# Decode attention beside a small dense block: a nested TensorE loop that works the V cache batch by batch

## The chip, the cores and the metric

One Trainium2 chip, one core. The metric is the device time of one execution in microseconds (us). It has a part outside the profiled span of the core (here 1.7 to 3 us).

## The reference, cut to what matters

Two batches, one query position, 32 heads, 4096 cached keys and values of 128 elements, all bf16. Attention (A) is mixed with a two-layer ReLU block (B) by a sigmoid gate.

```python
q = (x @ wq)                                            # 2 x 32 heads x 128
scores = jnp.einsum("bhqd,bhkd->bhqk", q, k_cache) * (128 ** -0.5)
p = softmax(scores)                                     # over 4096 keys
o = jnp.einsum("bhqk,bhkd->bhqd", p, v_cache)
a = o @ wo                                              # ... heads joined before
b = relu(x @ w1) @ w2
return g * a + (1 - g) * b                              # g = sigmoid(sum(x * gate_w))
```

K and V are 64 MiB each. They are read once, so the work is a stream of memory: 64 loads of 2 MB (two heads of one batch each), 32 of K and then 32 of V.

## The kernel before

A small recording layer keeps a list of instructions for each engine, works out the semaphore waits and emits them; TensorE's repeated parts stand in a loop of 8 turns of 4 loads. One queue (sync engine) issues all big loads into four slots of 2 MB, so that a load waits until TensorE is done with the load four places earlier:

```python
    def kv_in(n):                                       # load n: K for n < 32, then V
        c = A_k_cache if n < 32 else A_v_cache
        hp, b = divmod(n % 32, 2)                       # the two batches alternate
        return c[b, 2 * hp:2 * hp + 2].rearrange("h (p r) d -> (h p) r d", p=64)
    ...
    for n in range(64):
        waits = []
        if n >= NSLOT:                                  # NSLOT = 4
            prev = n - NSLOT
            waits.append(f"T_{prev}_7" if prev < 32 else f"pv_{prev - 32}")
        load(f"ld_kv_{n}", kv_sb[:, n % NSLOT, :, :], kv_in(n), waits=waits, sem=f"slot{n % NSLOT}")
```

In the K part TensorE transposes each load (64 transposes, evacuated by VectorE and ScalarE) and multiplies by q; the scores of both batches stay in PSUM. Then comes the turn from K to V: for each batch the row maximum, the exponential, 16 transposes of the probabilities back into PSUM; then the sums of both batches; and only then the pV loop. Each pV is 64 matmuls with a load of V as the stationary side and a column pair of probabilities (`pst`) as the moving side; VectorE stages `pst` (`stage_p`) and scales each result (`o_norm`).

```python
    for g in range(2):                                  # both batches before the first pV
        row_max(g)
        exps(g)
        ptrans(g)
    denom_l(0)
    stage_p(0)
    denom_l(1)
    for i in (2, 1, 3):
        stage_p(i)
    denom()                                             # sums and reciprocals of both batches
    P.begin_loop(NIT)
    for p in range(PER):
        PV(p)
    P.end_loop()
    for i in range(32):
        o_norm(i)
        if i + PER < 32:
            stage_p(i + PER)
    ...
    def stage_p(i):
        hp, g = divmod(i, 2)
        ...
        for hh in range(2):
            P.add("dve", lambda e, hh=hh: e.tensor_copy(out=pst[64 * hh:64 * hh + 64, p, :, hh], in_=src[:, :, 2 * hp + hh]),
                  waits=[f"pt_{g}", "c_ps"] + ([f"pv_{i - PER}"] if i >= PER else []),
                  signal=f"pst_{i}" if hh else None, sem=f"ps{p}")

    def o_norm(i):
        hp, g = divmod(i, 2)
        P.add("dve", lambda e: e.tensor_tensor(out=oT[:, g, 2 * hp:2 * hp + 2], in0=o_col(i % PER), in1=rg[:, g, 2 * hp:2 * hp + 2], op=ALU.mult),
              waits=[f"pv_{i}", f"rg_{g}"], signal=f"oT_{i}", sem=f"on{i % PER}")
```

(The sum, the gate and the output projection, whose weights are the last 4 MB to be loaded, are cut here.)

## Time and profile before

| | before |
|---|---|
| time at the prediction (3 runs) | 352.36 us median (351.13, 352.36, 573.64; the last is no fast run) |
| span of the profiled run | 349.2 us |
| bytes read | 145.4 MB |
| DMA rate in the K part, in the V part | 428, 429 GB/s |
| TensorE busy in the K part, in the V part | 99.7%, 39% |

The lines of the page of the kernel before that show this, in 40 equal slices of the span; the digits are the DMA engines' mean busy share in tenths, the numbers what they moved:

```profile
DMA  8999999999999999999999999999999999999994
GB/s 338 405 415 428 430 424 422 434 428 424 425 435 426 423 430 434 428 424 434 430 424 423 381 422 439 426 422 430 434 428 421 432 430 428 424 435 428 424 420 167
```

DMA is full from end to end. In slice 23 (192 to 201 us) the rate dips to 381 GB/s. The same place in stretches of 1 us, then the turn from K to V as a whole and the V part (columns: busy us with instruction counts of TensorE's matmuls, its weight loads, VectorE, ScalarE and GpSimd, then granted TensorE clock, DMA share, GB/s):

```profile
194.00:195.00 1.00, 1.00 (x44) 1.00 (x42) 0.33 (x2) 0.00 (x0) 0.00 (x0) 0.50 0.99 410
195.00:196.00 1.00, 1.00 (x43) 1.00 (x41) 0.53 (x3) 0.00 (x0) 0.00 (x0) 0.50 0.60 229
196.00:197.00 1.00, 0.63 (x24) 0.54 (x21) 0.00 (x0) 0.00 (x0) 0.00 (x0) 0.50 1.04 295
197.00:198.00 1.00, 0.98 (x35) 0.98 (x36) 0.53 (x3) 0.00 (x0) 0.00 (x0) 0.50 0.78 279
198.00:199.00 1.00, 1.00 (x44) 1.00 (x42) 0.00 (x0) 0.00 (x0) 0.00 (x0) 0.50 1.15 492
180.00:210.00 30.00, 18.64 (x465) 16.74 (x462) 13.28 (x52) 5.82 (x8) 0.00 (x0) 0.64 0.99 412
204.00:318.00 114.00, 43.91 (x1522) 42.52 (x1523) 12.54 (x72) 0.00 (x0) 0.00 (x0) 0.50 1.01 429
```

Three stretches from 195 to 198 us are at about two thirds of the rate; 412 against 428 GB/s over 30 us is 30 * (1 - 412/428) = 1.1 us. The cause is in the timeline of the kernel before (start, duration, engine, line, operation; the bracket is idle time and what ended it):

```profile
182.49 1.29 DVE L353 COPY kt_sb<-PS 128x1024 bf16<-128x1024 bf16 x2 [0.20 <-PE PS L326]
...
186.42 1.23 DVE L373 TENSOR_REDUCE m<-PS 128x1 f32<-128x1024 f32 x1
186.42 1.11 ACT L386 ACTIVATE E<-PS,negM 128x1024 bf16<-128x1024 f32 x1 [2.03 <-DVE negM L381]
...
187.68 1.18 PE L392 MATMUL PS<-ident,E 128*64 128x128 bf16 x16 [3.24 <-ACT E L386]
...
189.15 1.11 ACT L386 ACTIVATE E<-PS,negM 128x1024 bf16<-128x1024 f32 x1 [1.52 <-DVE negM L381]
...
190.41 1.91 PE L392 MATMUL PS<-ident,E 128*64 128x128 bf16 x16 [1.55 <-ACT E L386]
...
192.25 1.06 PE L402 MATMUL PS<-lm,ones 128*128 128x32 f32 x4
...
193.13 3.50 PE L433 MATMUL PS<-pst,kv_sb 128*128 128x2 bf16 x125
...
195.04 0.16 DVE L423 TENSOR_TENSOR oT<-PS,rg 128x2 bf16<-128x2 f32 x1 [0.70 <-PE PS L433]
```

The last K transposes are evacuated by 183.8 us. Batch 0's exponential runs at 186.4, its transposes at 187.7; then TensorE waits for batch 1's exponential (189.15), transposes it (190.4) and makes the sums (192.25). pV 0 is over at about 195.0, where VectorE scales it (the line at 195.04), and only then is the fifth V load issued. Each V load after that waits on TensorE for nothing: TensorE waits about 3 us for each load (lines of the timeline in the middle of V):

```profile
262.74 1.87 PE L433 MATMUL PS<-pst,kv_sb 128*128 128x2 bf16 x64 [2.96 <-DMA kv_sb<-in_A_v_cache_dram]
267.72 1.85 PE L433 MATMUL PS<-pst,kv_sb 128*128 128x2 bf16 x64 [3.11 <-DMA kv_sb<-in_A_v_cache_dram]
272.62 1.85 PE L433 MATMUL PS<-pst,kv_sb 128*128 128x2 bf16 x64 [3.05 <-DMA kv_sb<-in_A_v_cache_dram]
277.52 0.64 PE L433 MATMUL PS<-pst,kv_sb 128*128 128x2 bf16 x19 [3.05 <-DMA kv_sb<-in_A_v_cache_dram]
```

Three lines of the page's list of DMA queues, on which no reading rested at first and everything rests later:

```profile
q1 hardware_dynamic: 10488, 145.43, 98.4%
q8 instruction: 7, 0.11, 0.1%
q14 instruction: 5, 0.04, 0.0%
```

### The profile page before, as it was taken

The numbers are of one execution on the slowest core, as the hardware profiler recorded it, in microseconds if no ns is written. First come the engines' busy times: TensorE is split into PE (matmuls) and PEld (weight loads), VectorE is DVE, ScalarE is ACT, GpSimd is POOL, SyncE is SP. The second block draws the span as 40 slices with busy tenths as digits, with TensorE's granted clock in tenths as the row PEclk, the third lists the DMA queues.
The fourth block names the chain that finished last, engine by engine and source line by source line (L and its number), as shares of the span: only waits on it lengthen the run. The fifth ranks groups of instructions, "written<-read, shape, count | busy, mean of one in ns | idle before, by whom it ended". The sixth has DMA issues, their size and how long they took to land.

```text
span 349.2 us, 10866 instructions
## 1 busy us (share of the span) xinstructions
PE 236.4 (68%) x5019; PEld 202.6 (58%) x5019; DVE 132.0 (38%) x293; ACT 99.5 (28%) x105; POOL 12.0 (3%) x52
## 2 busy tenths in 40 slices
PE   2549999999999999999994933443244433443244
PEld 0549888787888788787883823443234423443233
DVE  1004766676766676666767311110111011110010
ACT  1004656565665566555763000000000000000000
POOL 5000000000000000000000000000000000000000
PEclk9999999999999999999997555555555555555555
DMA  8999999999999999999999999999999999999994
GB/s 338 405 415 428 430 424 422 434 428 424 425 435 426 423 430 434 428 424 434 430 424 423 381 422 439 426 422 430 434 428 421 432 430 428 424 435 428 424 420 167
DMA packets 10514, 145.59 MB, mean 417 GB/s; under 512 B 1187, under 2 KB 1286, under 8 KB 1670
## 3 DMA queue, kind: packets, MB, share of 16 engines
q1 hardware_dynamic: 10488, 145.43, 98.4%
q8 instruction: 7, 0.11, 0.1%
q14 instruction: 5, 0.04, 0.0%
q10 hardware_dynamic: 14, 0.00, 0.0%
HBM read 145.43 MB, written 0.00 MB: 416 GB/s over the span
## 4 chain that ended last, share of the span: by engine, by line
PE 51%; DMA 43%; DVE 2%; issue 2%; SPq 1%; ACT 0%; DVEq 0%
PE PS L326 35%; DMA kv_sb<-in_A_v_cache_dram 29%; PE PS L337 10%; DMA wo_sb<-in_A_wo_dram 7%; DMA kv_sb<-in_A_k_cache_dram 7%; PE PS L433 5%; SPq L236 1%; DVE m L373 1%; PE PS L392 1%; DVE kt_sb L353 0%; ACT E L386 0%; DVE mq L376 0%; DVE negM L381 0%; PE PS L402 0%; PE PS L484 0%
## 5 line engine op out<-in xcount | busy, mean ns | idle before, releaser
L326 PEld LDWEIGHTS PS<-ident,kv_sb 128*128 128x128 bf16 x2048 | 117.3, 99 | 18.7 <-issue 14.4
L326 PE MATMUL PS<-ident,kv_sb 128*128 128x128 bf16 x2048 | 124.2, 222 | 3.7 <-DMA kv_sb<-in_A_k_cache_dram 3.4
L353 DVE COPY kt_sb<-PS 128x1024 bf16<-128x1024 bf16 x160 | 105.4, 688 | 55.6 <-PE PS L326 55.6
L433 PE MATMUL PS<-pst,kv_sb 128*128 128x2 bf16 x2048 | 59.2, 165 | 85.8 <-DMA kv_sb<-in_A_v_cache_dram 82.4
L350 ACT ACTIVATE kt_sb<-PS 128x1024 bf16<-128x1024 bf16 x96 | 94.1, 1022 | 69.2 <-PE PS L326 69.2
L433 PEld LDWEIGHTS PS<-pst,kv_sb 128*128 128x128 bf16 x2048 | 57.4, 104 | 87.7 <-issue 69.0
L423 DVE TENSOR_TENSOR oT<-PS,rg 128x2 bf16<-128x2 f32 x32 | 5.1, 159 | 128.0 <-PE PS L433 128.0
L337 PE MATMUL PS<-kt_sb,qst 128*32 128x512 bf16 x512 | 38.2, 382 | 0.0
L337 PEld LDWEIGHTS PS<-kt_sb,qst 128*32 128x32 bf16 x512 | 13.3, 95 | 12.5 <-DVE kt_sb L353 3.6
L417 DVE COPY pst<-PS 64x64 bf16<-64x64 bf16 x64 | 14.3, 224 | 2.1 <-PE PS L392 1.4
L357 POOL COPY qst<-qmask 128x64 bf16<-128x64 bf16 x32 | 7.4, 237 | 151.7 <-PE PS L337 140.6
L484 PE MATMUL PS<-wo_sb,os_sb 128*2 128x128 bf16 x128 | 4.3, 305 | 3.2 <-DMA wo_sb<-in_A_wo_dram 3.2
L302 PE MATMUL PS<-xT_sb,wq_sb 128*128 128x2 bf16 x128 | 3.6, 165 | 4.2 <-DMA wq_sb<-in_A_wq_dram 4.2
L392 PE MATMUL PS<-ident,E 128*64 128x128 bf16 x32 | 3.1, 272 | 4.8 <-ACT E L386 4.8
L302 PEld LDWEIGHTS PS<-xT_sb,wq_sb 128*128 128x128 bf16 x128 | 3.5, 104 | 4.2 <-DMA wq_sb<-in_A_wq_dram 4.2
L392 PEld LDWEIGHTS PS<-ident,E 128*64 128x64 bf16 x32 | 2.6, 142 | 5.5 <-ACT E L386 5.5
L484 PEld LDWEIGHTS PS<-wo_sb,os_sb 128*2 128x2 bf16 x128 | 2.9, 112 | 4.4 <-DMA wo_sb<-in_A_wo_dram 2.2
L286 PE MATMUL PS<-ident,gw_sb 1*128 1x1 bf16 x4 | 0.3, 172 | 4.4 <-DMA gw_sb<-in_gate_w_dram 4.4
L386 ACT ACTIVATE E<-PS,negM 128x1024 bf16<-128x1024 f32 x2 | 2.2, 1113 | 3.6 <-DVE negM L381 3.6
L307 DVE TENSOR_SCALAR qmask<-PS 128x32 bf16<-128x32 f32 x2 | 0.5, 323 | 7.4 <-PE PS L302 7.4
L448 ACT ACTIVATE hr_sb<-PS 128x20 f32<-128x20 f32 x1 | 0.2, 187 | 10.2 <-PE PS L442 10.2
L516 DVE TENSOR_TENSOR out_sb<-PS,f_sb 98x128 bf16<-98x128 f32 x1 | 0.3, 291 | 7.2 <-PE PS L484 7.2
(51 smaller groups left out, 31.5 us busy)
## 6 DMA issues: line engine op xcount, KB each, us to landing
kv_sb<-in_A_k_cache_dram SPq DMA_DIRECT2D x32, 2048.0 KB, 14.5
kv_sb<-in_A_v_cache_dram SPq DMA_DIRECT2D x32, 2048.0 KB, 17.6
wq_sb<-in_A_wq_dram SPq DMA_DIRECT2D x1, 4096.0 KB, 12.4
wo_sb<-in_A_wo_dram SPq DMA_DIRECT2D x1, 2048.0 KB, 22.1
w_sb<-in_B_w_dram SPq DMA_DIRECT2D x1, 1376.0 KB, 15.3
w_sb<-in_B_w_dram SPq DMA_DIRECT2D x1, 1280.0 KB, 18.9
wo_sb<-in_A_wo_dram SPq DMA_DIRECT2D x1, 1024.0 KB, 24.1
wo_sb<-in_A_wo_dram SPq DMA_DIRECT2D x1, 512.0 KB, 24.9
```

Source lines behind the costliest of these rows:

```text
L236: P.add(eng, lambda e: e.dma_start(dst, src), waits=waits, signal=name, sem=sem or name, inc=16)
L302: P.add("pe", lambda e, h=h, t=t: e.matmul(bank(7, 2 * h, 2), lhsT=wq_sb[:, t, h * 128:(h + 1) * 128], rhs=xT_sb[:, t, :], start=(t == 0), ...
L326: P.add("pe", lambda e, iv, q=q, rr=rr, r=r: e.transpose(bank16(4 + q % 4, rr * 128, 128), kv_sb[:, p, r, :], ident16[:, :]), waits=waits ...
L337: P.add("pe", lambda e, iv, c=c, hh=hh: e.matmul(S_chunk(p % 2, c), lhsT=qst[:, p, hh, :], rhs=kt_sb[:, p % NKT, 8 * c:8 * c + 8, 64 * hh: ...
L350: P.add("act", lambda e, dst=dst, src=src: e.activation(out=dst, in_=src, func=ACT.Copy), waits=w, signal=f"ev_{i}_{q}", sem=f"ev{p}{q}")
L353: P.add("dve", lambda e, dst=dst, src=src: e.tensor_copy(out=dst, in_=src), waits=w, signal=f"ev_{i}_{q}", sem=f"ev{p}{q}")
L357: P.add("pool", lambda e: e.tensor_copy(out=qst[:, p, :, :], in_=qmask[:, 32 * (i % 2) + i // 2 * 2:32 * (i % 2) + i // 2 * 2 + 2, :]), wa ...
L392: P.add("pe", lambda e, k=k: e.transpose(PSB[0:64, 2048 * g + 128 * k:2048 * g + 128 * k + 128], E_sb[g][:, 64 * k:64 * k + 64], ident16[: ...
L417: P.add("dve", lambda e, hh=hh: e.tensor_copy(out=pst[64 * hh:64 * hh + 64, p, :, hh], in_=src[:, :, 2 * hp + hh]), waits=[f"pt_{g}", "c_p ...
L423: P.add("dve", lambda e: e.tensor_tensor(out=oT[:, g, 2 * hp:2 * hp + 2], in0=o_col(i % PER), in1=rg[:, g, 2 * hp:2 * hp + 2], op=ALU.mult ...
L433: P.add("pe", lambda e, iv, r=r, k=p_place(r): e.matmul(o_col(p), lhsT=kv_sb[:, p, r, :], rhs=pst[:, p, k, :], start=(r == 0), stop=(r == ...
L484: P.add("pe", lambda e, r=r, c=c: e.matmul(acc(c), lhsT=os_sb[:, r, :], rhs=wo_sb[:, r, 128 * c:128 * c + 128], start=(r == 0), stop=(r == ...
```

## The change

The intent is to start the first pV after the work of batch 0 alone, and to do batch 1's maximum and exponential on engines that are idle while V is streamed. V is then read in the order of batches: 16 loads of batch 0, 16 of batch 1. TensorE's program becomes a loop in a loop; the recording layer learns to nest loops. The probabilities of both batches use the same SBUF and PSUM tiles in turn. The zeroing of the score banks at the start becomes 4 matmuls instead of 16.

```diff
@@ recording layer (cut) @@
-        self.loop = None
+        self.loops = []
...
@@ kv_in @@
-        hp, b = divmod(n % 32, 2)
+        hp, b = divmod(n, 2) if n < 32 else (n % 16, n // 16 - 2)
@@ exps @@
-              waits=[f"negM_{g}"], signal=f"E_{g}")
+              waits=[f"negM_{g}"] + (["pt_0"] if g else []), signal=f"E_{g}", sem="E")
@@ ptrans (for both turns, in the loop) @@
-                  waits=[] if k else [f"E_{g}"], signal=f"pt_{g}" if k == 15 else None)
+                  waits=[] if k else (lambda g: [f"E_{g}"] + (["pst_15"] if g else [])),
+                  signal=(lambda g: f"pt_{g}") if k == 15 else None)
...
@@ stage_p, o_norm @@
-        hp, g = divmod(i, 2)
+        g, hp = divmod(i, 16)
@@ the order @@
-    for g in range(2):
-        row_max(g)
-        exps(g)
-        ptrans(g)
+    row_max(0)
+    exps(0)
     denom_l(0)
-    stage_p(0)
-    denom_l(1)
-    for i in (2, 1, 3):
-        stage_p(i)
-    denom()
-    P.begin_loop(NIT)
+    P.begin_loop(2)
+    ptrans()
+    denom_sum()
+    P.begin_loop(4)
     for p in range(PER):
         PV(p)
     P.end_loop()
-    for i in range(32):
-        o_norm(i)
-        if i + PER < 32:
-            stage_p(i + PER)
+    P.end_loop()
+    for g in range(2):
+        for k in range(PER):
+            stage_p(16 * g + k)
+        denom(g)
+        for i in range(16 * g, 16 * g + 16):
+            o_norm(i)
+            if i < 16 * g + 12:
+                stage_p(i + PER)
+            if i == 3:
+                row_max(1)
+                exps(1)
+                denom_l(1)
```

More of the change, by code (lines that the diff above doesn't have):

```diff
@@ L59, in add @@
         op = _Op(fn, waits, signal, sem or engine + "_ev", inc)
-        if engine == "pe" and self.loop is not None:
-            self.loop.ops.append(op)
+        if engine == "pe" and self.loops:
+            self.loops[-1].ops.append(op)
         else:
@@ L65, in begin_loop @@
     def begin_loop(self, n):
-        self.loop = _Loop(n)
-        self.streams["pe"].append(self.loop)
+        loop = _Loop(n)
+        (self.loops[-1].ops if self.loops else self.streams["pe"]).append(loop)
+        self.loops.append(loop)
     def end_loop(self):
-        self.loop = None
+        self.loops.pop()
     def _count(self, op, name, counts):
@@ L77, in _count, with _run @@
         self.marks[name] = (op.sem, counts[op.sem])
+    def _run(self, items, counts, u):
+        for it in items:
+            if isinstance(it, _Loop):
+                for t in range(it.n):
+                    self._run(it.ops, counts, (u or 0) * it.n + t)
+            elif it.signal is not None:
+                self._count(it, it.signal if u is None else it.signal(u), counts)
     def resolve(self):
@@ L81, in resolve @@
         for e in self.ENGINES:
-            for it in self.streams[e]:
-                if isinstance(it, _Loop):
-                    for t in range(it.n):
-                        for op in it.ops:
-                            if op.signal is not None:
-                                self._count(op, op.signal(t), counts)
-                else:
-                    self._count(it, it.signal, counts)
+            self._run(self.streams[e], counts, None)
     def _needs(self, names):
@@ L104, in _linear @@
             known = [(t, d[s]) for t, d in enumerate(per_t) if s in d]
-            b = 0 if len(known) == 1 else (known[1][1] - known[0][1]) // (known[1][0] - known[0][0])
+            t0, v0 = known[0]
+            b = (-(-v0 // t0) if t0 else 0) if len(known) == 1 else (known[1][1] - known[0][1]) // (known[1][0] - known[0][0])
             a = known[0][1] - b * known[0][0]
@@ L110, in _linear, with emit @@
         return out
-    def emit(self, engine, eng):
-        for it in self.streams[engine]:
+    def emit(self, engine, eng, items=None, iv=None, total=1):
+        vals = {}
+        for it in self.streams[engine] if items is None else items:
             if isinstance(it, _Loop):
-                lin = [self._linear(op, it.n) for op in it.ops]
-                with eng.Fori(0, it.n) as iv:
-                    vals = {}
-                    for ws in lin:
-                        for _, a, b in ws:
-                            if b and (a, b) not in vals:
-                                vals[(a, b)] = eng.snap(iv * b + a)
-                    for op, ws in zip(it.ops, lin):
-                        for s, a, b in ws:
-                            eng.wait_ge(self.sem(s), vals[(a, b)] if b else a)
-                        ins = op.fn(eng, iv)
-                        if op.signal is not None:
-                            ins.then_inc(self.sem(op.sem), op.inc)
-            else:
-                for s, v in self._needs(it.waits).items():
-                    eng.wait_ge(self.sem(s), v)
-                ins = it.fn(eng)
-                if it.signal is not None:
-                    ins.then_inc(self.sem(it.sem), it.inc)
+                with eng.Fori(0, it.n) as k:
+                    self.emit(engine, eng, it.ops, k if iv is None else iv * it.n + k, total * it.n)
+                continue
+            if iv is None:
+                waits = list(self._needs(it.waits).items())
+            else:
+                waits = []
+                for s, a, b in self._linear(it, total):
+                    if b and (a, b) not in vals:
+                        vals[(a, b)] = eng.snap(iv * b + a)
+                    waits.append((s, vals[(a, b)] if b else a))
+            for s, v in waits:
+                eng.wait_ge(self.sem(s), v)
+            ins = it.fn(eng)
+            if it.signal is not None:
+                ins.then_inc(self.sem(it.sem), it.inc)
 def bass_gated_mix__gqa_block_cached__dense_activation_relu__decode_kernel(
@@ L174, in bass_gated_mix__gqa_block_cached__dense_activation_relu__decode_kernel @@
     qst = sb("qst", [128, PER, 2, 32], b16)
-    E_sb = [sb(f"E{g}", [128, 1024], b16) for g in range(2)]
+    E_sb = sb("E_sb", [128, 1024], b16)
     pst = sb("pst", [128, PER, 64, 2], b16)
@@ L181, in bass_gated_mix__gqa_block_cached__dense_activation_relu__decode_kernel @@
     l4 = sb("l4", [128, 2], f32)
-    lm = sb("lm", [128, 2, 32], f32)
+    lm = sb("lm", [128, 32], f32)
     rinv = sb("rinv", [128, 2, 32], f32)
@@ L274, in bass_gated_mix__gqa_block_cached__dense_activation_relu__decode_kernel @@
     P.add("dve", lambda e: e.memset(zt[:], 0.0), signal="c_zt")
-    for g in range(2):
-        for c in range(8):
-            P.add("pe", lambda e, g=g, c=c: e.matmul(S_chunk(g, c), lhsT=zt[:, 0:32], rhs=zt[:, :], start=True, stop=True,
-                                                     tile_position=(0, 32 * (c % 4)), skip_group_check=True),
-                  waits=["c_zt"] if c + g == 0 else [])
+    for k in range(4):
+        P.add("pe", lambda e, k=k: e.matmul(bank(k, 0, 512), lhsT=zt[:, 0:128], rhs=zt[:, :], start=True, stop=True),
+              waits=["c_zt"] if k == 0 else [])
     for t in range(4):
@@ L324, in waits @@
                     return w + (["qm_0", "qm_1", "f_sb"] if p == 0 and q == 0 else [])
-                P.add("pe", lambda e, iv, q=q, rr=rr, r=r: e.transpose(bank16(4 + q % 4, rr * 128, 128), kv_sb[:, p, r, :], ident16[:, :]),
+                P.add("pe", lambda e, q=q, rr=rr, r=r: e.transpose(bank16(4 + q % 4, rr * 128, 128), kv_sb[:, p, r, :], ident16[:, :]),
                       waits=waits if rr == 0 else [],
@@ L335, in waits @@
                     return ([f"qst_{i}"] if c == 0 else []) + ([f"ev_{i}_{c}"] if c >= 4 else [])
-                P.add("pe", lambda e, iv, c=c, hh=hh: e.matmul(
+                P.add("pe", lambda e, c=c, hh=hh: e.matmul(
                     S_chunk(p % 2, c), lhsT=qst[:, p, hh, :], rhs=kt_sb[:, p % NKT, 8 * c:8 * c + 8, 64 * hh:64 * hh + 64],
@@ L385, in exps @@
     def exps(g):
-        P.add("act", lambda e: e.activation(out=E_sb[g][:, :], in_=S_region(g), func=ACT.Exp, bias=negM[:, g:g + 1], scale=1.0,
+        P.add("act", lambda e: e.activation(out=E_sb[:, :], in_=S_region(g), func=ACT.Exp, bias=negM[:, g:g + 1], scale=1.0,
                                             accum_out=l4[:, g:g + 1]),
-              waits=[f"negM_{g}"], signal=f"E_{g}")
-    def ptrans(g):
+              waits=[f"negM_{g}"] + (["pt_0"] if g else []), signal=f"E_{g}", sem="E")
@@ L391, in ptrans @@
+    def ptrans():
         for k in range(16):
-            P.add("pe", lambda e, k=k: e.transpose(PSB[0:64, 2048 * g + 128 * k:2048 * g + 128 * k + 128],
-                                                   E_sb[g][:, 64 * k:64 * k + 64], ident16[:, :]),
-                  waits=[] if k else [f"E_{g}"], signal=f"pt_{g}" if k == 15 else None)
+            P.add("pe", lambda e, k=k: e.transpose(PSB[0:64, 128 * k:128 * k + 128], E_sb[:, 64 * k:64 * k + 64], ident16[:, :]),
+                  waits=[] if k else (lambda g: [f"E_{g}"] + (["pst_15"] if g else [])),
+                  signal=(lambda g: f"pt_{g}") if k == 15 else None)
@@ L396, in denom_l @@
     def denom_l(g):
-        P.add("dve", lambda e: e.tensor_scalar(out=lm[:, g, :], in0=jmask[:, :], scalar1=l4[:, g:g + 1], scalar2=None, op0=ALU.mult),
-              waits=[f"E_{g}", "c_j4"], signal=f"lm_{g}")
-    def denom():
-        for g in range(2):
-            P.add("pe", lambda e, g=g: e.matmul(bank(MISC, 32 * g, 32), lhsT=ones[:, :], rhs=lm[:, g, :], start=True, stop=True),
-                  waits=[f"lm_{g}", "c_one"], signal="lb" if g else None)
-        P.add("dve", lambda e: e.reciprocal(out=rinv[:, :, :], in_=bank(MISC, 0, 64).rearrange("p (g j) -> p g j", g=2)),
-              waits=["lb"], signal="rinv")
-        for g in range(2):
-            P.add("dve", lambda e, g=g: e.tensor_scalar(out=rg[:, g, :], in0=rinv[:, g, :], scalar1=g_sb[:, g:g + 1], scalar2=None,
-                                                        op0=ALU.mult),
-                  waits=["rinv", "g"], signal=f"rg_{g}")
+        P.add("dve", lambda e: e.tensor_scalar(out=lm[:, :], in0=jmask[:, :], scalar1=l4[:, g:g + 1], scalar2=None, op0=ALU.mult),
+              waits=[f"E_{g}", "c_j4"] + (["lb_0"] if g else []), signal=f"lm_{g}", sem="lm")
@@ new lines, in denom_sum, with denom @@
+    def denom_sum():
+        P.add("pe", lambda e: e.matmul(bank(MISC, 0, 32), lhsT=ones[:, :], rhs=lm[:, :], start=True, stop=True),
+              waits=lambda g: [f"lm_{g}", "c_one"] + (["rinv_0"] if g else []), signal=lambda g: f"lb_{g}")
+    def denom(g):
+        P.add("dve", lambda e: e.reciprocal(out=rinv[:, g, :], in_=bank(MISC, 0, 32)), waits=[f"lb_{g}"], signal=f"rinv_{g}")
+        P.add("dve", lambda e: e.tensor_scalar(out=rg[:, g, :], in0=rinv[:, g, :], scalar1=g_sb[:, g:g + 1], scalar2=None, op0=ALU.mult),
+              waits=[f"rinv_{g}", "g"], signal=f"rg_{g}")
@@ L412, in stage_p @@
     def stage_p(i):
-        hp, g = divmod(i, 2)
+        g, hp = divmod(i, 16)
         p = i % PER
-        src = PSB[0:64, 2048 * g:2048 * g + 2048].rearrange("p (k j) -> p k j", j=32)
+        src = PSB[0:64, 0:2048].rearrange("p (k j) -> p k j", j=32)
         for hh in range(2):
@@ L421, in o_norm @@
     def o_norm(i):
-        hp, g = divmod(i, 2)
+        g, hp = divmod(i, 16)
         P.add("dve", lambda e: e.tensor_tensor(out=oT[:, g, 2 * hp:2 * hp + 2], in0=o_col(i % PER), in1=rg[:, g, 2 * hp:2 * hp + 2],
@@ L432, in waits @@
                 return [f"ld_kv_{32 + i}", f"pst_{i}"] + ([f"oT_{i - 2}"] if i >= 2 else [])
-            P.add("pe", lambda e, iv, r=r, k=p_place(r): e.matmul(o_col(p), lhsT=kv_sb[:, p, r, :], rhs=pst[:, p, k, :],
+            P.add("pe", lambda e, r=r, k=p_place(r): e.matmul(o_col(p), lhsT=kv_sb[:, p, r, :], rhs=pst[:, p, k, :],
                                                                     start=(r == 0), stop=(r == 63)),
@@ L495, in bass_gated_mix__gqa_block_cached__dense_activation_relu__decode_kernel @@
         evac(i)
-    for g in range(2):
-        row_max(g)
-        exps(g)
-        ptrans(g)
+    row_max(0)
+    exps(0)
     denom_l(0)
-    stage_p(0)
-    denom_l(1)
-    for i in (2, 1, 3):
-        stage_p(i)
-    denom()
-    P.begin_loop(NIT)
+    P.begin_loop(2)
+    ptrans()
+    denom_sum()
+    P.begin_loop(4)
     for p in range(PER):
```

## The prediction

> **What bounds it now.** The DMA stream. The page's 40-slice table shows DMA at 9 in almost every slice; the table of stretches gives 428 GB/s at 30-180 us (K, TensorE 99.7% busy but keeping pace) and 429 at 204-318 us (V, TensorE 39% busy).[...] In V a 2 MB load lands every 4.9 us and its 64 pV matmuls take 1.86 us (timeline), so TensorE, VectorE and the half granted clock have 3 us to spare per load. The change removes no byte.
>
> **The only slack it can win** is at the turn from K to V. Four slots of 2 MB are in flight; the fifth V load waits for the first pV. Timeline: the last K transposes end about 182.9 us; exponential of batch 0 at 186.4, its transposes 187.7; then batch 1's (maximum 186.4, exponential 189.15, transposes 190.4-192.3), two sums (192.3-193.3), pV 0 done 195.04. The queue runs thin meanwhile: by 1 us stretches, 195-198 us shows 229, 295 and 279 GB/s against 428, about 480 KB short, = 1.1 us; 180-210 us averages 412, which also gives 30*(1-412/428) = 1.1 us. Everywhere else DMA is full.
>
> **What the change does.**
> - Takes batch 1's maximum (2.7 us with its small steps), exponential (1.3), 16 transposes (1.9) and one sum (0.5) out from before pV 0. Estimate from those durations: transposes of batch 0 187.7-188.9, sum to 189.8, pV 0 done about 191.9 instead of 195.0. The fifth V load is issued 3 us sooner, before the queue thins. Worth at most the hole, 1.1 us.
> - Moves batch 1's maximum and exponential after the fourth pV: about 4.2 us of VectorE, which idles over 4 us per load. Nothing visible.
> - Puts between pV 15 and 16: loop branch (0.4 us as at other turns), 16 transposes at half clock (1.9), sum (1, beside the first staging copies 0.46). About 3.3 us[...], against 3 us in which TensorE would wait for the load anyway. pV 16 comes 0.3 to 2.5 us late, and one V load is issued that late; but 3 loads (over 12 us) are in flight. Cost: none.
> - V is read batch by batch in address order instead of alternating. I expect no change of rate; small unknown either way.
> - Fewer zeroing matmuls at the start: TensorE waits 3.4 us for the first K load there, so nothing. Tail (projection weights, 25 us) unchanged.
>
> **Predicted time.** The two normal runs of before are 351.13 and 352.36; I start from about 352.1 and take 1.1 off: 351.0 us. Range 349.8 to 352.5. Faster by over 2%: 1%; within 2%: 98%; slower: 1%.
>
> **What would show it.** (1) First pV over near 192 us, and the 1 us stretches of 190-200 us all near 428 GB/s. (2) V pace unchanged: 19.6 us per four loads. (3) At pV 16 no wait on DMA; transposes and sum stand in its place, and DMA share in the 20 us after stays at 1.0. (4) K ends at the same 182-184 us. (5) Span shorter by about 1 us.
>
> **What would make it wrong.** The hole may not be one of missing loads (then the 1.1 us stays). The turn of the outer loop may cost over 12 us (then the queue dries in the middle of V). Reading V in sequence may change the DMA rate: 1% of 31 loads is 1.5 us. TensorE sits within 1% of being the limit in K[...]. Run-to-run spread (0.3%) is as large as the effect.

The sum of the time is 352.1 - 1.1 = 351.0 us. The turn between pV 15 and 16 was put at 0.4 + 1.9 + 1 = 3.3 us and entered the sum with 0; the 2.5 of "0.3 to 2.5 us late" is no more than the author's estimate. For the 0.4, the trace of before shows 0.44 to 0.58 us from the branch of the loop to the next weight load at the seven turns of K. That DMA bounds the kernel rests on the rates alone: 428 GB/s with TensorE 99.7% busy and 429 with it 39% busy; how far that is from what the DMA engines could move was not shown.

## The result, and the profile after

| | before | after |
|---|---|---|
| time, median of 6 runs | 351.23 us | 350.90 us (350.67 to 350.95) |
| ratio of fast runs, 95% interval | | 0.9984 (0.997 to 0.9998) |
| span of the profiled run | 349.2 us | 349.2 us |
| DMA rate, 180 to 210 us | 412 GB/s | 426 GB/s |

A ratio is the mean time of one kernel's fast runs over that of the other's of the same rounds, so not quite the ratio of the medians. Both kernels pass the comparison with the reference (which doesn't notice V heads that are put in the wrong place).

The time is inside the predicted range. But the predicted gain was 1.1 us, and the measured one is 0.0016 * 351 = 0.6 us with an interval from nothing to about 1; and the two profiled spans, which hold the same work, do not differ at all. Yet the hole is gone. The same stretches of the kernel after:

```profile
194.00:195.00 1.00, 0.00 (x0) 0.00 (x0) 0.00 (x0) 0.00 (x0) 0.00 (x0) 0.50 1.03 426
195.00:196.00 1.00, 0.00 (x0) 0.00 (x0) 0.00 (x0) 0.00 (x0) 0.00 (x0) 0.50 1.04 442
196.00:197.00 1.00, 0.80 (x30) 0.80 (x30) 0.00 (x0) 0.00 (x0) 0.00 (x0) 0.50 0.92 393
197.00:198.00 1.00, 0.40 (x16) 0.32 (x12) 0.53 (x3) 0.00 (x0) 0.00 (x0) 0.50 1.08 459
198.00:199.00 1.00, 0.78 (x30) 0.81 (x31) 0.00 (x0) 0.00 (x0) 0.00 (x0) 0.50 1.00 426
180.00:210.00 30.00, 16.92 (x470) 15.20 (x466) 13.28 (x53) 5.78 (x8) 0.00 (x0) 0.65 1.01 426
204.00:318.00 114.00, 45.42 (x1511) 43.71 (x1509) 13.37 (x72) 0.61 (x2) 0.00 (x0) 0.50 1.01 428
```

The timeline of the kernel after shows every step of the mechanism in its place: the transposes of batch 0 at 187.7, the sum at 188.7, pV 0 over by 191.6, batch 1's maximum and exponential at 200.7 and 203.4 beside the pV of batch 0:

```profile
182.45 1.29 DVE L352 COPY kt_sb<-PS 128x1024 bf16<-128x1024 bf16 x2 [0.20 <-PE PS L325]
...
186.38 1.11 ACT L385 ACTIVATE E_sb<-PS,negM 128x1024 bf16<-128x1024 f32 x1 [2.03 <-DVE negM L380]
...
187.72 1.08 PE L391 MATMUL PS<-ident,E_sb 128*64 128x128 bf16 x16 [3.32 <-ACT E_sb L385]
...
188.72 0.52 PE L400 MATMUL PS<-lm,ones 128*128 128x32 f32 x2
...
189.43 4.24 PE L430 MATMUL PS<-pst,kv_sb 128*128 128x2 bf16 x153 [0.18 <-DVE pst L414]
...
191.61 0.16 DVE L420 TENSOR_TENSOR oT<-PS,rg 128x2 bf16<-128x2 f32 x1
...
200.67 1.23 DVE L372 TENSOR_REDUCE m<-PS 128x1 f32<-128x1024 f32 x1
...
203.40 1.11 ACT L385 ACTIVATE E_sb<-PS,negM 128x1024 bf16<-128x1024 f32 x1 [15.82 <-DVE negM L380]
```

So 1.1 us was given back somewhere. The pV in the middle of V show where (timeline of the kernel after, TensorE alone; compare the four lines of before, which start 4.9 us apart):

```profile
259.01 1.91 PE L391 MATMUL PS<-ident,E_sb 128*64 128x128 bf16 x16 [0.22 <-issue]
...
260.85 0.64 PE L400 MATMUL PS<-lm,ones 128*128 128x32 f32 x2
...
261.76 1.87 PE L430 MATMUL PS<-pst,kv_sb 128*128 128x2 bf16 x64 [0.27 <-DMA kv_sb<-in_A_v_cache_dram]
...
266.74 1.84 PE L430 MATMUL PS<-pst,kv_sb 128*128 128x2 bf16 x64 [3.12 <-DMA kv_sb<-in_A_v_cache_dram]
...
272.59 1.85 PE L430 MATMUL PS<-pst,kv_sb 128*128 128x2 bf16 x64 [4.01 <-DMA kv_sb<-in_A_v_cache_dram]
...
277.48 1.85 PE L430 MATMUL PS<-pst,kv_sb 128*128 128x2 bf16 x64 [3.04 <-DMA kv_sb<-in_A_v_cache_dram]
```

The turn of the outer loop costs nothing: transposes and sum fit between pV 15 and the load that pV 16 needs. But from 266.74 to 272.59 there are 5.85 us where there should be 4.9, and all later loads are late by as much. The page's slices show no dip there:

```profile
DMA  8999999999999999999999999999999999999993
GB/s 327 413 423 420 428 428 424 425 434 428 423 432 435 419 424 435 432 420 428 434 430 420 427 434 422 426 432 432 422 432 423 434 422 432 432 428 422 432 416 128
```

Slice 31 (262 to 271 us) moved 423 GB/s, slice 32 434. A load is 0.95 us late, and the DMA rate does not show it.

### What the landing records show

A look below the views explains this. Each of the 64 loads has 16 completion records in the trace, as many as the page counts DMA engines. TensorE starts on a load when the last of the 16 is there: those of the fifth V load after the change lie between 200.63 and 202.98 us, and TensorE starts on it at 203.02. So it is with V loads 4 to 31 of both kernels: the first weight load comes 0.04 to 0.11 us after the last record (0.36 us for V 4 before), though the last but one is there up to 1.6 us earlier.

Take from each record the time at which a steady stream would land it: 24.3 us + 4.8935 us * n for load n of the 64 (the first record of load 0 is at 24.33 us before, 24.41 after, and the first records of V loads 4 to 31 are 4.893 us apart in both traces). What is left I read as how far one DMA engine lags. The records do not name the engine, but the sixteen values hardly change from one load to the next (from V 19 to V 31 none of them moves by more than 0.02 us from one load to the next), so that one can follow them. Values in us, sorted; V 3 is the last V load issued before the first pV; "last" is the landing that TensorE waits for:

```
before      last     lag of the 16 engines
V 3       197.74   0.03 0.11 0.19 0.26 0.28 0.35 0.66 0.72 0.75 0.76 1.49 1.62 1.66 1.77 1.94 2.16
V 4       203.88   1.54 1.60 1.65 1.65 1.66 1.68 1.69 1.77 1.81 1.90 1.92 1.94 2.01 2.23 2.25 3.41
V 17      267.59   1.55 1.59 1.63 1.65 1.68 1.68 1.72 1.78 1.79 1.88 1.92 1.95 2.24 2.30 3.44 3.51
V 18      272.48   1.55 1.59 1.62 1.65 1.67 1.69 1.71 1.77 1.79 1.88 1.91 1.95 2.29 3.19 3.44 3.51
V 31      336.13   1.54 1.60 1.62 1.65 1.68 1.72 1.76 1.79 1.83 1.89 1.96 1.97 2.33 3.23 3.47 3.54

after
V 3       198.09   0.17 0.19 0.21 0.28 0.29 0.30 0.31 0.39 0.79 1.23 1.55 1.82 1.88 1.89 1.91 2.51
V 4       202.98   0.17 0.21 0.28 0.29 0.30 0.32 0.40 0.79 1.22 1.55 1.82 1.88 1.88 1.89 1.91 2.51
V 17      266.60   0.18 0.22 0.29 0.29 0.31 0.35 0.40 0.79 1.27 1.56 1.74 1.82 1.89 1.90 1.92 2.52
V 18      272.45   0.17 0.22 0.28 0.29 0.31 0.34 0.41 0.78 1.27 1.55 1.73 1.82 1.89 1.90 1.92 3.48
V 31      336.10   0.16 0.25 0.29 0.31 0.33 0.37 0.41 0.83 1.29 1.56 1.75 1.82 1.89 1.90 1.93 3.51
```

Two things are to be seen.

- The hole before (V 3 to V 4) sets back the ten engines that were ahead: they stood at 0.03 to 0.76 us, and after it none stands below 1.54. The engine that lagged by 2.16 us still had work when the next load was issued (issue at 195.03 us, its record of V 3 at 197.74) and loses nearly nothing (2.23 or 2.25).
- The seven foremost engines of the kernel after end 1.3 to 1.4 us ahead of those of before. The slowest does not: it jumps from 2.52 to 3.48 us between V 17 and V 18 and ends at 3.51, where the slowest of before ends at 3.54. TensorE starts at the last record, and so the end is the same (336.13 and 336.10 us).

What sets an engine back? The DMA records of the trace have instruction transfers, the two lines "q8" and "q14" of the queue list above, of 16 KB and 8 KB. The records of both kernels during the run, in us from the start:

```
              q8 (16 KB)                                          q14 (8 KB)
before        18.2  25.1  37.0  44.8  194.6  201.4  223.4         63.2  93.0  115.6  186.5  268.3
after         18.2  26.6  37.0  46.1  193.5  200.2  342.6         63.4  92.9  115.7  193.0  267.4
```

The q14 transfer at 267.35 us takes 0.325 us itself, and the data packet of 16 KB that starts as it ends, at 267.66, takes 1.273 us in place of the usual 0.614 (the median of all 16 KB packets). Together that is 0.325 + 0.66 = 0.98 us, if both are on one engine (the packets do not name it either), the size of the jump, and it comes between V 17 and V 18. A q8 transfer in the V part sets its engine back by about 1.5 us (that at 223.4 us before: from 1.96 us at V 8 to 3.49 at V 9). What it costs depends on where that engine stood: before, the two at 201 and 223 us strike engines at about 1.9 us, which the hole has put there, and these two are the slowest at the end (3.47 and 3.54); after, the one at 200 us strikes an engine at 0.19, which goes to 1.88 and never matters. In both tables no lag shrinks by more than about 0.1 us from V 4 to V 31. All five 8 KB transfers of each kernel in this list are on q14, and each is followed at once by a slow data packet of q1 (0.96 to 1.27 us); the 16 KB ones are on q8.

This is a theory made after the fact. It makes numbers, and those could be tested.

### The profile page after: what moved, and what is told of

Read it like the earlier page. It is cut to its first block, busy times and chain, and to the rows that moved or that the text cites. A ratio compares the mean times of both kernels' runs of the same rounds, so it can differ in the third digit from the quotient of the medians.

```text
span 349.2 us, 10856 instructions
## 1 busy us (share of the span) xinstructions
PE 236.3 (68%) x5007; PEld 202.7 (58%) x5007; DVE 132.8 (38%) x294; ACT 99.5 (28%) x105; POOL 12.0 (3%) x52
## 4 chain that ended last, share of the span: by engine, by line
PE 49%; DMA 49%; SPq 1%; issue 1%; DVE 0%
PE PS L325 35%; DMA kv_sb<-in_A_v_cache_dram 35%; PE PS L336 10%; DMA wo_sb<-in_A_wo_dram 7%; DMA kv_sb<-in_A_k_cache_dram 7%; PE PS L430 4%; SPq L237 1%; PE PS L481 0%; DVE out_sb L518 0%
## 5 line engine op out<-in xcount | busy, mean ns | idle before, releaser
L385 ACT ACTIVATE E_sb<-PS,negM 128x1024 bf16<-128x1024 f32 x2 | 2.2, 1113 | 17.8 <-DVE negM L380 17.8
L391 PE MATMUL PS<-ident,E_sb 128*64 128x128 bf16 x32 | 3.0, 266 | 3.5 <-ACT E_sb L385 3.3
L391 PEld LDWEIGHTS PS<-ident,E_sb 128*64 128x64 bf16 x32 | 2.6, 139 | 4.1 <-issue 4.1
```

Of the source, the lines that this page charges most:

```text
L391: P.add("pe", lambda e, k=k: e.transpose(PSB[0:64, 128 * k:128 * k + 128], E_sb[:, 64 * k:64 * k + 64], ident16[:, :]), waits=[] if k else ...
```

## The experiments

**First theory (slowest DMA engine).** The end of the stream is set by the engine with the largest lag. Filling the hole helps the engines that it had set back, the two slowest of the kernel before among them; but the engine that takes three 8 KB instruction transfers gains nothing by it, and after the change it is the slowest. **Rivals:** the hole is worth its 1.1 us and the small gain is scatter; the new order of V costs DMA rate and eats the gain; the turn of the outer loop costs time (this one the lines above settle: pV 16 still waits for its load). Ten runs were made, one of them of the changed kernel itself.

### The changed kernel once more

No edit.

> The changed kernel once more, for a tighter ratio and a second trace. First theory (slowest DMA engine): a load has landed when the last of the 16 DMA engines has written its part, so idle time of the other 15 costs nothing. The landing records of the two traces put the lag of the slowest engine at the last V load at 3.54 us before and 3.51 us after, though the hole of 1.1 us is gone: the gain is then 0 to 0.4 us, ratio 0.999 to 1.000. Second theory (the hole is worth its full 1.1 us and the first measurement was scatter): ratio 0.9969.

Measured: 350.76 us median against 351.12 of 11 runs of before on the same chip, ratio 0.9993 (0.998 to 1.0005). The mean span of the 5 runs is 349.02 us, that of the 11 runs of before 349.11. So in the span the change is worth about 0.1 us, in this second set too. The lag of the slowest engine at the last V load is 3.75 us this time; the jump between V 17 and V 18 is again 0.97. The 0.9969 of the "second theory" (the hole counts in full) is outside the interval.

### Fewer VectorE instructions, in the kernel after and in the kernel before

The same edit in both. The two staging copies stand one behind the other in VectorE's list and wait for the same things, so that the waits of the second are left out; the constant `c_ps` is waited for once, and `rg` once for each batch. This takes 93 separate wait instructions out of VectorE's program (107 to 14 in the traces), all in the V part:

```diff
-                  waits=[f"pt_{g}", "c_ps"] + ([f"pv_{i - PER}"] if i >= PER else []),
+                  waits=[] if hh else [f"pt_{g}"] + (["c_ps"] if i == 0 else []) + ([f"pv_{i - PER}"] if i >= PER else []),
...
-              waits=[f"pv_{i}", f"rg_{g}"], signal=f"oT_{i}", sem=f"on{i % PER}")
+              waits=[f"pv_{i}"] + ([f"rg_{g}"] if hp == 0 else []), signal=f"oT_{i}", sem=f"on{i % PER}")
```

> The changed kernel with about 100 redundant VectorE wait instructions taken out of the V part. First theory: the instruction transfers seen in the DMA records (8 KB each, one at 267 us, when the slowest engine's lag jumps from 2.52 to 3.48 us) are what the slowest engine loses; if that one belongs to VectorE's program it goes away or moves by tens of us, and if it goes the time falls by 0.9 to 1.0 us, to about 349.9. Second theory: waits on an engine with over 3 us to spare per load cost nothing, same time as the changed kernel within 0.15 us.

> The same wait instructions taken out of the kernel before. First theory: there the engine that takes the 8 KB transfers ends at a lag of 3.2 us, two others (16 KB instruction transfers at 201 and 223 us) at 3.45 and 3.54, so taking its transfer away is masked: gain 0 to 0.1 us, although the same edit gains 0.9 or more in the changed kernel. Second theory: no gain in either.

Measured, on one chip with the run above:

| | time, us | ratio to before (95%) | mean span, us |
|---|---|---|---|
| before | 351.12 | | 349.11 |
| after | 350.76 | 0.9993 (0.998 to 1.0005) | 349.02 |
| before, fewer waits | 350.82 | 1.0002 (0.9987 to 1.0017) | 349.02 |
| after, fewer waits | 349.75 | 0.9967 (0.9956 to 0.9979) | 347.80 |

Each edit alone is worth 0.1 us of span; both together 1.3 us. In the trace of the fourth kernel the transfer at 267 us is gone (the one after 192 us comes at 348.7, after the span; every trace has one there), and no load is late (its timeline, TensorE in the middle of V):

```profile
261.34 1.87 PE L430 MATMUL PS<-pst,kv_sb 128*128 128x2 bf16 x64 [0.30 <-DMA kv_sb<-in_A_v_cache_dram]
266.33 1.84 PE L430 MATMUL PS<-pst,kv_sb 128*128 128x2 bf16 x64 [3.12 <-DMA kv_sb<-in_A_v_cache_dram]
271.22 1.84 PE L430 MATMUL PS<-pst,kv_sb 128*128 128x2 bf16 x64 [3.05 <-DMA kv_sb<-in_A_v_cache_dram]
276.11 1.85 PE L430 MATMUL PS<-pst,kv_sb 128*128 128x2 bf16 x64 [3.04 <-DMA kv_sb<-in_A_v_cache_dram]
```

Its largest lag at the last V load is 2.12 us. In the third kernel the transfer near 268 us is gone as well, but two other engines end at 3.23 and 3.46 us: those that stood at 1.6 to 1.9 us after the hole and then took a 16 KB transfer, at 201 and 222.6 us. There the hole is in the way; its rate at the turn is that of the kernel before:

```profile
180.00:210.00 30.00, 19.08 (x481) 17.05 (x474) 13.22 (x52) 5.95 (x8) 0.00 (x0) 0.64 0.99 413
```

This is what the first theory had said of the two kernels. It also gives the worth of the change where VectorE's third transfer doesn't mask it: from 350.82 to 349.75, 1.07 us (1.22 in the mean span). That this is so near to the predicted 1.1 is partly chance: the profiled spans differ by 1.34, as the largest lags do (3.46 and 2.12), and these depend on which engines the 16 KB transfers strike. The change also moved one of these from 223 us to 342; no run takes that apart, but without it the slowest engine here would be the one at 3.23, so by these lags it is worth 0.2 us at most.

### The program made long again, without the waits

A rival for the last result: fewer waits made VectorE and with it the release of slots faster. So 100 tiny memsets were put into VectorE's idle time between pV 5 and pV 12.

```diff
+            if i in (5, 7, 9, 11):
+                for k in range(25):
+                    P.add("dve", lambda e, k=k, i=i: e.memset(pad[:, 25 * (i // 2 - 2) + k:25 * (i // 2 - 2) + k + 1], 0.0))
             if i == 3:
                 row_max(1)
```

> The version without the redundant waits, with 100 tiny VectorE memsets put into VectorE's idle time between pV 5 and pV 12, so that its program is as long again as in the changed kernel while the waits stay out. First theory: the third 8 KB transfer on the slowest engine comes back near 265 us, that engine's lag jumps by 0.95 us and the time goes back to about 350.7 (ratio to before 0.999). Rival (taking the waits away sped VectorE and with it the release of slots): time stays at 349.75 (ratio 0.9965).

Measured: 350.60 us, ratio 0.9987 (0.9974 to 1.0001), mean span 348.84 (before on the same chip: 349.07). Of the 1.3 us of span, 1.0 is gone again. The other 0.2 to 0.3 us stay open; the slowest engine also starts V less behind in these two traces (2.13 and 2.10 us at V 3) than in the two of the changed kernel (2.51 and 2.78). This run and the one it is set against were made on different chips, and their intervals touch, so the reading rests on the trace. The transfer is back, not near 265 us as expected but at 233.9, since the memsets stand earlier in the program; the load that lands next is late by 0.96 us (timeline, TensorE):

```profile
232.10 1.85 PE L431 MATMUL PS<-pst,kv_sb 128*128 128x2 bf16 x64 [3.05 <-DMA kv_sb<-in_A_v_cache_dram]
237.94 1.85 PE L431 MATMUL PS<-pst,kv_sb 128*128 128x2 bf16 x64 [4.00 <-DMA kv_sb<-in_A_v_cache_dram]
242.75 1.87 PE L431 MATMUL PS<-pst,kv_sb 128*128 128x2 bf16 x64 [2.96 <-DMA kv_sb<-in_A_v_cache_dram]
```

From 232.10 to 237.94 is 5.84 us. The lag of one engine goes from 2.13 to 3.09 us and ends at 3.11. For the microsecond in question the rival falls: it is the length of VectorE's program, not its waits.

### Whose transfers they are

The changed kernel with instructions added that do nothing useful: first on four engines at once, then on one alone.

```diff
+    for k in range(10):                                  # VectorE, at the start
+        P.add("dve", lambda e, k=k: e.memset(pad[:, k:k + 1], 0.0))
+    for k in range(12):                                  # GpSimd, at the start
+        P.add("pool", lambda e, k=k: e.memset(pad[:, 16 + k:17 + k], 0.0))
+    for k in range(12):                                  # ScalarE, after the ReLU
+        P.add("act", lambda e, k=k: e.activation(out=pad[:, 32 + k:33 + k], in_=g_sb[:, 0:1], func=ACT.Copy), waits=["g"] if k == 0 else [])
+            for k in range(3):                           # sync engine, before load 4
+                P.add("sp", lambda e: e.wait_ge(P.sem("ld_x"), 16))
```

> Only to tell which engine's program each 8 KB instruction transfer belongs to. 10 tiny instructions more on VectorE (two loads' worth, its transfers about 10 us earlier), 12 on GpSimd (six loads' worth, about 29 us earlier), 12 on ScalarE (four loads' worth, about 20 us earlier), 3 waits on the sync engine (three loads, about 15 us earlier). Each of the transfers near 63, 93, 116, 193 and 267 us should move by one of these four amounts. If none moves, they are not fetches of program text and the first theory loses its cause for the lags.

> The changed kernel with only the 10 VectorE memsets of the earlier padded run. That run moved the transfer of 193 us to 178 us, which fits 3 sync-engine waits (14.7 us) and also VectorE's 10 instructions. If the transfer at 193 us belongs to VectorE's program, as the same DMA engine being hit at 63, 193 and 267 us suggests, it moves to about 178 us here and the one at 63 us to about 54; the ones near 93 and 116 us stay.

> The changed kernel with only the 3 sync-engine waits. If the transfer at 193 us belongs to VectorE's program, nothing moves: 63, 93, 116, 193, 267 us, each within 1 us. If it belongs to the sync engine's, it moves to about 178 us here and stays in the run with VectorE's 10 memsets.

Measured, the q14 transfers in us:

```
after, second trace     63.1   93.7  115.8  193.8  267.6
all four padded         54.1   74.1   86.5  178.1  265.3
VectorE alone           54.7   93.3  115.4  177.5  264.7
sync engine alone       63.2   93.2  115.8  193.9  267.1
```

The transfers near 63, 193 and 267 us belong to VectorE's program, that near 93 us fits ScalarE's shift and that near 116 us GpSimd's. The first run alone would have put the one at 193 us down to the sync engine, as its shift of 15 us fits the three waits; the two single runs show that this was wrong. VectorE's three hit one and the same DMA engine, as far as the lags can be followed: about 0.5 us, then 1.5, 2.5, 3.5, so each costs it about 1.0 us; those at 93 and 116 us set an engine back by 0.6 to 0.7 us. Whose the 16 KB transfers (q8) are was not tested. None of the three padded times tells anything: 351.16, 350.72 and 351.09 us, single runs of unknown state.

### V in the old order

```diff
-        hp, b = divmod(n, 2) if n < 32 else (n % 16, n // 16 - 2)
+        hp, b = divmod(n % 32, 2)
```

The result is wrong: the loads hold other heads than the probabilities.

> The changed kernel with V read in the old order, alternating between the batches (result wrong on purpose). If the new order cost DMA rate and ate the gain, this is 0.5 us or more faster than the changed kernel (350.2 or less). First theory: no difference, 350.8 within 0.3, the interval between landings 4.89 us in both.

Measured: 350.50 us (350.43 to 350.56), ratio 0.9983 (0.9967 to 0.9998). This lies at the edge of what was expected. Landings are 4.89 us apart, as in the changed kernel, and the one late load (+0.89 us at V 18) is there. The largest lag ends at 3.10 instead of 3.51 or 3.75 us, as its engine starts V 0.4 to 0.7 us less behind. So the order of V does not cost the stream its rate; whether the 0.3 us of the time are more than the scatter of such starts stays open.

### A larger hole

The transposes of batch 0 are repeated before the loop, with the same data, which only delays pV 0.

```diff
+    for k in range(48):                                  # and in a second kernel 96
+        P.add("pe", lambda e, k=k: e.transpose(PSB[0:64, 128 * (k % 16):128 * (k % 16) + 128], E_sb[:, 64 * (k % 16):64 * (k % 16) + 64], ident16[:, :]),
+              waits=[] if k else ["E_0"])
     P.begin_loop(2)
     ptrans()
```

> The changed kernel with the transposes of batch 0 made four times over instead of once (48 more of them, correct result), so pV 0 is over at about 196.3 us instead of 191.2, later than the 195.0 of the kernel before. If a hole counts in full: the missing bytes are 2.4 us worth, time +2.4 us against the changed kernel (353.2). First theory: the engine that sets the landings is 2.5 us behind and loses nothing; the others fall back to 2.4 to 3 us and one of them takes a 16 KB transfer (1.5 us) after it, so the end is at a lag of about 4.2 instead of 3.5: +0.7 us (351.5).

> The same with 96 more transposes, pV 0 over at about 202 us. Now every engine runs dry, and both theories have the time grow one for one from here: about 5.7 us over the run with 48 (357.2 by the first theory, 358.9 if a hole counts in full).

Measured: 351.33 us (350.69 to 352.58) and 354.16 us (352.59 to 355.25). The delays were smaller than planned: the granted clock, 0.50 in the stretches from 190 to 192 us (48) and 188 to 191 us (96), went up to 1.00 within the next 1 to 2 us while TensorE still had these transposes to do (90 and 73 ns each in the mean, 4.34 us for 48 and 7.01 for 96, where the 16 of batch 1 before took 1.91 us, 119 ns each, at a clock of 0.50), so that pV 0 was over by 195.9 and 198.7 us. The holes follow from the rate between 180 and 210 us, first with 48, then with 96:

```profile
180.00:210.00 30.00, 19.82 (x483) 18.21 (x480) 13.07 (x51) 5.84 (x8) 0.00 (x0) 0.70 0.98 404
```

```profile
180.00:210.00 30.00, 21.57 (x510) 19.67 (x498) 13.16 (x51) 6.16 (x8) 0.00 (x0) 0.80 0.89 362
```

As 30 * (1 - rate/428), and with the span of the same profiled run (each row is one execution):

| kernel | hole, us | span, us | longer than after (349.2) by | largest lag at the last V load |
|---|---|---|---|---|
| after | 0.1 | 349.2 | | 3.51 |
| before | 1.1 | 349.2 | 0.0 | 3.54 |
| 48 more transposes | 1.7 | 349.7 | 0.5 | 4.06 |
| 96 more transposes | 4.6 | 352.3 | 3.1 | 6.65 |

About the first 1.2 to 1.5 us of a hole are free, and what goes beyond is paid nearly in full. The expected numbers of the first theory were off (0.7 us for 48 fits, 357.2 us for 96 does not), because the delays themselves were; set against the holes that really came about, a hole that counts in full doesn't fit these profiles, and the first theory does. The scatter between runs of these two kernels is large, 2 to 3 us.

### One number for all runs

The span less the largest lag at the last V load is 349.20 - 3.54 = 345.66 us before, 345.66 after, 345.55 in the second trace of after, 345.57 in both kernels with fewer waits, and 345.66, 345.67, 345.66 and 345.67 for the program made long again, the old order, 48 and 96. With VectorE alone padded it is 345.57. In the two runs with extra sync-engine waits it is 346.0, for a reason that stays open. In the other ten profiles the span is the lag of the slowest DMA engine plus a constant, to 0.1 us, while the spans themselves go from 347.7 to 352.3. The lag at V 31 is that landing less a fixed number (332.6 us), so this says one thing and no more: what follows the last landing of V takes the same 13 us in all ten. That single engines decide this landing is what the tables above show.

## Why the prediction was right or wrong

- **The time, 351.0 us predicted, 350.9 measured: right**, in part by luck. The start, "about 352.1", was too high: it leaned on one run of 352.36, and the median of before over 11 later runs is 351.12. Some of the slower runs are longer mostly outside the span (for example 351.68 us with a span of 349.1, where 350.61 us has 348.8). A start that was 1 us too high and a gain that was too large cancelled.
- **What bounds it: right in kind, too coarse.** It is the DMA stream, but not its mean rate: it is the slowest of its 16 engines. A share of 1.0 and 428 GB/s hide 2.0 us (before) and 3.4 us (after) between the first and the last engine at the end of V (1.4 us at load 0 in both).
- **The hole, its cause and its filling: right.** pV 0 was expected over at 191.9 us and is over by 191.6; the ten stretches from 190 to 200 us have a DMA share of 0.99 and 415 GB/s in the mean (0.96 and 383 before), and K ends where it did. That each would be near 428 did not come out: single ones go from 328 to 516.
- **"Worth at most the hole, 1.1 us", and then "take 1.1 off": this step failed.** As the size of the gain it did not hold: missing bytes were counted as time one for one, although the time hangs on whichever engine is last at the end (lag 3.54 us before, 3.51 after). In the span the change brought 0.0 us (profiles) to 0.1 us (means), in the time 0.2 to 0.6 us. The missing microsecond was lost to the third instruction transfer of VectorE on a DMA engine that already lagged. That is shown by taking it away in both kernels: the change is then worth 1.07 us.
- **The turn between pV 15 and 16: right that it costs nothing, and cheaper than said.** It was said that pV 16 would come 0.3 to 2.5 us late with no wait on DMA; in fact transposes and sum are over at 261.5 us, and pV 16 still waits 0.27 us for its load.
- **"Everywhere else DMA is full" and "V pace unchanged: 19.6 us per four loads": right for the rate, wrong for one load,** the 5.85 us at V 18.
- **Batch 1's maximum and exponential beside pV, fewer zeroing matmuls, the tail: right,** none shows in the time. **Order of V: no change of rate,** as expected.

## What to carry to other kernels

Where a kernel is bound by DMA and never lets the queues run dry, look at when the last of the 16 parts of a load lands, not at the mean rate: whatever held up one DMA engine here stayed until the end (0.96 us at V 18, still there at V 31), and a short dry spell was free up to 1.2 to 1.5 us. The length of an engine's instruction list was then a cost, as the padded runs show that its transfers go over the same DMA engines: here 93 waits less on an engine that idles most of the time, together with the change, gave 0.33% (349.75 us, the best version that was run). When a filled hole brings less than it should, compare landing times load by load in both traces before you blame the new order of work.
